# Band attention into a gated feed-forward: a unit's two query tiles laid into the two halves of the partition rows

## The chip, the cores and the metric

The kernel runs on one core of a Trainium2 chip. The metric is the time of one execution in microseconds (us), measured on the device. TensorE is called PE, its weight loads PEld, VectorE DVE, ScalarE ACT, GpSimd POOL, and the engine that issues the DMAs SP.

## What is computed

For 4 batches of 8 heads with 768 positions and 64 dimensions per head, every position attends to the 4 first positions (the sinks) and to itself and the 127 positions ahead of it; then a gated feed-forward runs over the 3072 tokens of 512 values. Everything is float32.

```python
scores = scale * q @ k.T                     # per batch and head, 768 x 768
keep = (pos < n_sink) | ((0 <= rel) & (rel < window))
a = softmax(where(keep, scores, -1e9))
x = (a @ v), heads side by side              # 3072 x 512
out = (sigmoid(x @ w_gate) * (x @ w_val)) @ w_out     # d_ff = 1536
```

## The kernel before, in words

**Units.** The attention is cut into 96 units: `AT` gives three groups of T = 2 query tiles (128 queries each) per batch, and `attend` (line 719) handles one head of one group. A tile's keys are those of its own 128 positions, those of the 128 ahead, and 16 sink columns; `KW` = 144 is one stored key tile with its sinks, so a score tile has 272 columns, or 144 where the tile is the first of its sequence (`n`, line 756). The host hands q and k over transposed, head dimension first.

**Plain and split units.** The first `PLAIN` = 16 units multiply in full float32: each matmul then shows as two records in the trace. The other 80 split each operand into a rounded part (type fp32r, which TensorE multiplies in one pass) and the rest, and add up products of parts. `load` (line 701) brings q and k into the tile `qkT`: a plain unit once, into rows 0 to 63; a split unit twice, into rows 0 to 63 and 64 to 127, so with four DMAs, and one more for v.

**Scores of a split unit** (lines 738 to 749 and 758 to 765). `copy` and `rest` make `qs` (rounded q in the upper 64 rows, the rest of q in the lower 64), `kh` (rounded k in both halves) and `kl` (rest of k in both halves). With all 128 rows contracted, `qs` x `kh` and `qs` x `kl` together hold all four products. So a score tile is two matmuls over 128 rows:

```python
pairs = (qs, kh), (qs, kl)
PE.matmul(sc()[:, 0:n], lhsT=qq()[0:K, t*128 : t*128+128],
          rhs=kk()[0:K, s0 : s0+n], ...)      # K = 64 if plain else 128
```

Each of the two tiles of a unit is a planner operation of its own (line 781) with its own PSUM bank of the ring `a` (`B_a` = 3). After it come mask and row minimum on DVE (`top`), the exponential on ACT (`exp`), the reciprocal of the row sums (`rs`), the multiplication of `P` by it tile by tile (lines 797 to 811), the sink part (`st`, `turned`, `sk`), the transposes of P on TensorE (`turn`), two band cuts on POOL (`split`), and the product with v (`pv`). The result goes to `XH` and `XL`, the rounded part and the rest of x, which hold 6 tiles (`RING`).

**Feed-forward.** `feed` and `feed_part` (lines 1089 and 1119) work on chunks of 2 or 3 tiles (`MT`). Chunk 0 uses the weights in float32; its x lies in the tiles `X0`, which borrow the buffers of `qs`, `kh`, `kl` and `vhl` (line 987). Later chunks use three fp32r products per weight block: matmuls `m<-XH,ws`, `m<-XL,ws` for gate and value, and `o<-ws,gh`, `o<-wol,gh`, `o<-ws,gl` for the output.

**Order.** `Plan` (line 256) is a list scheduler that runs while the kernel is built. Every operation has a priority and, for each engine that could do it, a cost in ns; the plan decides which engine does it, in which order each engine works, and which buffer a tile gets. On TensorE attention operations come first (priority = unit number), feed-forward operations fill the rest (`pe`, from 10000 up), and until 130 us of planned time extra matmuls on the identity (`warm`, `m<-ident`) fill up a stretch that has too little work. The engines then run these fixed orders and wait for one another by semaphores. All instructions of the plan carry line 489, so the groups below are told apart by tile names.

Of the kernel before, what the change touches and what calls it, by code (L numbers as in the profile page):

```python
# [20 lines left out]
NS = 16  # L21
# [27 lines left out]
UPS = 2  # L49
B_vraw = 2  # L50
B_turned = 3
B_qs = 2
B_kh = 2
B_vhl = 3
B_P = 2
B_w = 2
DNG = 0
ADDG = 0
# [15 lines left out]
BUFS = {}  # L74

@with_exitstack
def general(ctx, tc, q, k, v, ident, nsk, win, wres, wol_d, out):

    nc = tc.nc
    B, H, D, S = q.shape  # L80
    NT = S // 128
    DO = out.shape[1]
    NF = len(wres)
# [28 lines left out]
    with tc.For_i(0, B, 1) as b:  # L112
        with tc.For_i(0, H, 1) as h:
# [4 lines left out]
                )  # L118
            )
            qT = c1.tile([D, S], F32, name="gqT")  # L120
            nc.sync.dma_start(
                out=qT, in_=q[bass.ds(b, 1), bass.ds(h, 1)].rearrange("b h d s -> d (b h s)")
            )
            kT = c1.tile([D, S], F32, name="gkT")
            nc.sync.dma_start(
                out=kT.rearrange("d (t p) -> d t p", t=NT),
                in_=k[bass.ds(b, 1), bass.ds(h, 1)].rearrange(
                    "b h d (t p) -> d (b h t) p", t=NT
                )[:, :, 0:128],
            )  # L130
            for t in range(NT):
                sc = c2.tile([128, S], F32, name="g_sc")
                a = c2.tile([128, S], F32, name="g_a")
# [302 lines left out]
def kernel(  # L436
    ctx: ExitStack,
    tc: tile.TileContext,
    q: bass.AP,
    k: bass.AP,  # L440
    v: bass.AP,
    n_sink: bass.AP,
    window: bass.AP,
# [7 lines left out]
    w_gate, w_val, w_out = (  # L451
        w.bitcast(I32).rearrange("r (c w) -> r c w", w=2) for w in (w_gate, w_val, w_out)
    )
    B, H, D, S = q.shape
    DM, DF, _ = w_gate.shape
    DO = w_out.shape[1]
    NC = DM // 128
# [1 line left out]
    SCALE = 1.0 / float(D) ** 0.5  # L459
    NT = S // 128  # L460
    KW = 128 + NS

    keep = ctx.enter_context(tc.tile_pool(name="keep", bufs=1))
    wp = ctx.enter_context(tc.tile_pool(name="wp", bufs=1))
# [39 lines left out]
    def mac(cols):  # L504
        return max(cols * 13 / 12 / 2.4, 104.5) + 2.5

    def dma(prio, ns, fn, r=(), w=()):
        plan.op(prio, [("Q", 460, fn)], r, w, dma=ns)
# [43 lines left out]
    def tile(shape, dtype, tag, bufs, pool=None):  # L552
        return Tile(pool or p1, shape, dtype, tag, bufs)
# [144 lines left out]
            copy(u, H // 2 * D, hi, x, [raw], [(VSHL, i)])  # L698
            rest(u, H // 2 * D, lambda hs=hs: VSHL()[:, hs, D : 2 * D], x, hi, [raw], [(VSHL, i)])

    def load(u, b, h, t0, T, prev, L, vraw, qkT, plain):

        W, k0 = T * 128, (t0 - prev) * 128
        for part, src, o, n in ((0, k, (t0 - prev) * KW, L * KW), (2, q, t0 * 128, W)):
            at = 0 if part else W
            for i in range(1 if plain else 2):
                dma(
                    u, 0.75 * n, lambda i=i, src=src, o=o, n=n, at=at: Q.dma_start(
                        out=qkT()[i * D : i * D + D, at : at + n],
                        in_=src[b, h, :, o : o + n],  # L710
                    ), w=[(qkT, part + 4 * i)],
                )
        dma(
            u, 182.0 * L, lambda: Q.dma_start(
                out=vraw(), in_=v[b, h, k0 : k0 + L * 128].rearrange("(l p) d -> p l d", p=128)
            ), w=[vraw],
        )

    def attend(u, b, h, t0, T, XR):
# [6 lines left out]
            sinks(b, u)  # L726
        plain = u < PLAIN
        vraw = tile([128, L, D], F32, "vraw", BUFS["vraw"])
        qkT = tile([128, W + L * KW], F32, "qkT", BUFS["turned"])
        qT = lambda: qkT()[:, 0:W]  # L730
        kTf = lambda: qkT()[:, W : W + L * KW]
        load(u, b, h, t0, T, prev, L, vraw, qkT, plain)
        kk2, qq2 = [(qkT, 0), (qkT, 4)], [(qkT, 2), (qkT, 6)]
        if plain:
            pairs = ((qT, kTf),)
            qk_reads, qk_ns = [qkT], 4
        else:
            qs = tile([128, W], F32R, "qs", BUFS["qs"])
            kh = tile([128, L * KW], F32R, "kh", BUFS["kh"])
            kl = tile([128, L * KW], F32R, "kl", BUFS["kh"])  # L740
            copy(u, W, qs, qT, qq2, [qs])
            copy(u, L * KW, kh, kTf, kk2, [kh])
            rest(
                u, W, lambda: qs()[D:128], lambda: qT()[D:128], lambda: qs()[D:128],
                qq2 + [qs], [qs],
            )
            rest(u, L * KW, kl, kTf, kh, kk2 + [kh], [kl])
            pairs = (qs, kh), (qs, kl)
            qk_reads, qk_ns = [qs, kh, kl], 2

        P = tile([128, T, KW], F32, "P", BUFS["P"])
        rs = tile([128, 4], F32, "rs", BUFS["P"])
        for t in range(T):
            sc = tile([128, 512], F32, "a", BUFS["a"], ps)
            first = t0 + t == 0
            n = KW if first else KW + 128

            def qk(t=t, sc=sc, n=n):
                s0 = max(t + prev - 1, 0) * KW
                K = D if plain else 128  # L760
                for i, (qq, kk) in enumerate(pairs):
                    PE.matmul(
                        sc()[:, 0:n], lhsT=qq()[0:K, t * 128 : t * 128 + 128],
                        rhs=kk()[0:K, s0 : s0 + n], start=i == 0, stop=i == len(pairs) - 1,
                    )

            def top(t=t, sc=sc, first=first):
                if not first:
                    V.copy_predicated(out=sc()[:, 0:128], mask=tri, data=sc()[:, KW : KW + 128])
                V.tensor_tensor_reduce(  # L770
                    out=P()[:, t], in0=sc()[:, 0:KW], in1=am[min(t0 + t, 2)], op0=ALU.add,
                    op1=ALU.min, scale=-SCALE, scalar=3.0e38, accum_out=negm_all[:, u, t : t + 1],
                )

            def exp(t=t):
                A.activation(
                    out=P()[:, t], in_=P()[:, t], func=AF.Exp, bias=negm_all[:, u, t : t + 1],
                    scale=-1.0, accum_out=rs()[:, t : t + 1],
                )

            plan.op(u, [("PE", 10 + qk_ns * mac(n), qk)], qk_reads, [sc, (P, t)], busy=0.5 if plain else 0.9)
            plan.op(
                u, [("V", 290 if first else 600, top)],
                [sc, (MASKS, 3), (MASKS, min(t0 + t, 2))], [sc, (P, t)],
            )
            plan.op(u, [("A", 460, exp)], [], [(P, t), (rs, t)])
# [7 lines left out]
        plan.op(  # L794
            u, [("V", 120, lambda: V.reciprocal(out=rs()[:, 0:T], in_=rs()[:, 0:T]))], [], [rs]
        )
        for t in range(T):
            plan.op(
                u, [
                    ("V", 390, lambda t=t: V.tensor_scalar(  # L800
                        out=P()[:, t], in0=P()[:, t], scalar1=rs()[:, t : t + 1], scalar2=None,
                        op0=ALU.mult,
                    )),
                    ("A", 320, lambda t=t: A.mul(out=P()[:, t], in_=P()[:, t], mul=rs()[:, t : t + 1])),
                    ("G", 450, lambda t=t: G.tensor_scalar(
                        out=P()[:, t], in0=P()[:, t], scalar1=rs()[:, t : t + 1], scalar2=None,
                        op0=ALU.mult,
                    )),
                ][::-1],
                [rs], [(P, t)],  # L810
            )

        if not plain:
            st = tile([128, T, 2, NS], F32R, "st", BUFS["st"])
            turned = tile([128, T, 2 * NS], F32, "turned", BUFS["st"])
            sk = tile([128, T, 4, 32], F32R, "sk", BUFS["sk"])
            sinkw = lambda: P()[:, :, 128:KW]
            copy(u, 2 * T * NS, lambda: st()[:, :, 0], sinkw, [P], [(st, 0)])  # L820
            rest(
                u, T * NS, lambda: st()[:, :, 1], sinkw, lambda: st()[:, :, 0], [P, (st, 0)], [(st, 1)]
            )
            plan.op(
                u, [("V", 180, lambda: V.transpose(
                    out=turned().rearrange("p t x -> p (t x)"),
                    in_=st().rearrange("p t z x -> p (t z x)").bitcast(F32),
                ))],
                [st], [turned],
            )  # L830
            spread = lambda E: lambda: E.tensor_tensor(
                out=sk(), in0=turned().unsqueeze(2).broadcast_to([128, T, 4, 32]),
                in1=own.unsqueeze(1).unsqueeze(3).broadcast_to([128, T, 4, 32]), op=ALU.mult,
            )
            plan.op(
                u, [("G", pool(W), spread(G)), ("V", vec(W), spread(V))], [turned, OWN], [sk]
            )

        tp = tile([128, 512], F32, "a", BUFS["a"], ps)
# [130 lines left out]
        if h % 2:  # L970
# [8 lines left out]
            for run in runs:  # L979
# [5 lines left out]
                whole = chunk_of[g + run[0]] < WHOLE  # L985
                if whole:
                    X0[c] = tile([128, W], F32, *(
                        (("qs", BUFS["qs"]), ("kh", BUFS["kh"]), ("kl", BUFS["kh"]), ("vhl", BUFS["vhl"]))[c]
                    ))
                    copy(u, W, X0[c], x, [xr], [X0[c]], plain)  # L990
                    continue
# [266 lines left out]
    main.close()  # L1258
    flagged = nc.values_load(total[0:1, 0:1], min_val=0, max_val=512)
    with tc.If(flagged > 0):  # L1260
        general(tc, q, k, v, ident, nsk, win, wres, wol_d, out)


_INS = ["q", "k", "v", "n_sink", "window", "moe_w_gate", "moe_w_val", "moe_w_out"]
_OUTS = [((3072, 512), "float32")]


# [35 lines left out]
```

## Time and profile before

| | |
|---|---|
| time, median of 3 runs | 821.65 us (820.0 to 822.29) |
| time of the profiled execution | 821.27 us |
| its span, first to last instruction | 819.3 us |
| mean granted TensorE clock | 0.988 |
| busy: PE, PEld | 801.7 us, 706.3 us |
| busy: DVE, POOL, ACT | 529.1 us, 470.0 us, 420.1 us |

Matmuls are pipelined: the duration that the trace gives for one runs until its last result is written, while the next one has long begun. What a matmul occupies is read from the distance between the starts of two neighbours. The granted clock is a share of 2.4 GHz.

### The profile page before, as it was taken

What the parts mean: (1) busy time and instruction counts of PE and PEld (TensorE: products, weight loads), DVE (VectorE), ACT (ScalarE), POOL (GpSimd) and SP (SyncE); (2) the same over time, 40 slices, a digit from 0 to 9 for tenths busy, and PEclk for the clock granted to TensorE, in tenths of its full rate; (3) what the DMA queues carried; (4) which work ended last, traced back from release to release, by engine and by line L of the source; (5) the groups of instructions that cost most, each with busy time, mean ns of one, the idle gap of its engine ahead of it and who ended that gap; (6) DMA issues with size and microseconds to landing.
All of it is one profiled execution on the core that took longest, in us unless ns stands there. A gap on an engine that the chain in (4) does not pass through costs nothing.

```text
span 819.3 us, 14819 instructions
## 1 busy us (share of the span) xinstructions
PE 801.7 (98%) x4472; PEld 706.3 (86%) x4472; DVE 529.1 (65%) x1659; ACT 420.1 (51%) x1232; POOL 470.0 (57%) x666
## 2 busy tenths in 40 slices
PE   7999999999999999999999999999999999999997
PEld 5666576789999999999899988899899999999996
DVE  4668787988888888786951499956961495111111
ACT  4667777766677777654730377734640373001001
POOL 3467788787777777664851488755751474111111
PEclk7899999999999999999999999999999999999999
DMA  5567796454454553334341243433441141112112
GB/s 166 152 175 231 206 275 205 110 149 126 130 157 119 144 130 94 107 105 116 103 113 40 66 137 86 134 100 97 104 119 38 50 109 27 48 34 88 40 38 68
DMA packets 101013, 92.93 MB, mean 113 GB/s; under 512 B 47680, under 2 KB 82496, under 8 KB 100928
## 3 DMA queue, kind: packets, MB, share of 16 engines
q1 hardware_dynamic: 100928, 91.93, 40.4%
q8 instruction: 38, 0.62, 0.3%
q14 instruction: 47, 0.39, 0.1%
HBM read 82.45 MB, written 9.44 MB: 112 GB/s over the span
## 4 chain that ended last, share of the span: by engine, by line
PE 67%; DVE 8%; POOL 2%; ACT 2%; DMA 1%; issue 1%; SPq 0%; POOLq 0%; DVEq 0%; ACTq 0%
PE m L489 39%; PE o L489 19%; PE a L489 9%; DVE rs L489 1%; DMA qkT<-in_k_dram 1%; DVE P L489 1%; DVE st L489 1%; DVE gl L489 1%; POOL kl L489 1%; DVE xr L489 1%; DVE a L489 1%; ACT P L489 1%; DVE low L489 1%; DVE th L489 0%; POOL wt L489 0%
## 5 line engine op out<-in xcount | busy, mean ns | idle before, releaser
L489 PE MATMUL m<-XH,ws 128*128 128x384 f32 (+1 forms) x1536 | 399.7, 325 | 0.2 <-DVE th L489 0.2
L489 PEld LDWEIGHTS m<-XH,ws 128*128 128x128 f32 x1536 | 273.9, 188 | 2.9 <-DVE th L489 0.4
L489 PE MATMUL m<-XL,ws 128*128 128x384 f32 (+1 forms) x768 | 247.6, 322 | 0.0
L489 DVE SCALAR_TENSOR_TENSOR th<-th,m 128x384 f32<-128x384 f32 (+1 forms) x108 | 54.6, 505 | 193.5 <-PE m L489 190.3
L489 POOL TENSOR_TENSOR gl<-th,gh 128x384 fp32r<-128x384 f32 (+1 forms) x61 | 61.4, 1006 | 188.9 <-DVE gh L489 183.5
L489 ACT ACTIVATE th<-m 128x384 f32<-128x384 f32 (+1 forms) x108 | 49.1, 455 | 222.5 <-PE m L489 221.5
L489 PEld LDWEIGHTS m<-XL,ws 128*128 128x128 f32 x768 | 144.9, 189 | 2.5
L489 POOL TENSOR_SCALAR_AFFINE_SELECT wt<-wt 128x512 fp32r<-128x512 f32 (+3 forms) x192 | 121.1, 631 | 33.4 <-DVE wt L489 13.7
L489 PE MATMUL o<-ws,gh 128*128 128x512 f32 x264 | 106.4, 403 | 0.0
L489 PE MATMUL o<-ws,gl 128*128 128x512 f32 x264 | 104.3, 395 | 0.7 <-DVE gl L489 0.4
L489 PE MATMUL o<-wol,gh 128*128 128x512 f32 x264 | 103.2, 391 | 0.0
L489 ACT ACTIVATE P<-P,negm_all 128x144 f32<-128x144 f32 x192 | 78.9, 411 | 29.5 <-DVE negm_all L489 24.3
L489 DVE CUSTOM_DVE_ANT_0 P<-a,am 128x144 f32<-128x144 f32 x192 | 58.3, 305 | 7.9 <-PE a L489 2.2
L489 PEld LDWEIGHTS o<-ws,gl 128*128 128x128 f32 x264 | 49.5, 188 | 14.6 <-DVE gl L489 1.8
L489 ACT ACTIVATE P<-P,rs 128x144 f32<-128x144 f32 x114 | 44.1, 410 | 22.5 <-DVE rs L489 22.1
L489 PEld LDWEIGHTS o<-wol,gh 128*128 128x128 f32 x264 | 49.7, 188 | 5.7
L489 PEld LDWEIGHTS o<-ws,gh 128*128 128x128 f32 x264 | 49.7, 188 | 5.2
L489 POOL TENSOR_TENSOR qs<-qkT,qs 64x256 fp32r<-64x256 f32 x57 | 44.4, 779 | 16.0 <-issue 4.5
L489 POOL TENSOR_TENSOR kl<-qkT,kh 128x432 fp32r<-128x432 f32 (+1 forms) x45 | 50.1, 1112 | 3.9 <-ACT kh L489 2.0
L489 PE MATMUL a<-wt,vhl 128*128 128x256 f32 (+1 forms) x216 | 49.2, 330 | 0.5 <-POOL wt L489 0.3
L489 DVE COPY_PREDICATED a<-tri,a 128x128 f32<-128x128 int32 x160 | 45.4, 284 | 6.2 <-PE a L489 5.5
L489 PE MATMUL a<-kh,qs 128*128 128x272 f32 (+1 forms) x160 | 46.5, 295 | 1.1 <-DVE wt L489 0.5
(129 smaller groups left out, 1460.2 us busy)
## 6 DMA issues: line engine op xcount, KB each, us to landing
wol<-wol_d SPq DMA_DIRECT2D x96, 256.0 KB, 2.8
qkT<-in_k_dram SPq DMA_DIRECT2D x120, 108.0 KB, 2.7
qkT<-in_q_dram SPq DMA_DIRECT2D x176, 64.0 KB, 2.4
wst<-in_moe_w_gate_dram SPq DMA_DIRECT2D x12, 512.0 KB, 4.4
wst<-in_moe_w_val_dram SPq DMA_DIRECT2D x12, 512.0 KB, 4.1
wst<-in_moe_w_out_dram SPq DMA_DIRECT2D x12, 512.0 KB, 4.6
vraw<-in_v_dram SPq DMA_DIRECT2D x64, 96.0 KB, 2.3
out_dram<-w SPq DMA_DIRECT2D x23, 256.0 KB, 2.3
```

Of the source, the lines that this page charges most:

```text
L489: return lambda *a, **kw: tc.keep_in_program_order(op(*a, **kw))
```

## The change

One planner operation `qk_` now makes the scores of both tiles of a unit. The host lays out one array `qk`: per batch, head and pair of tiles 128 rows of 400 columns; rows 0 to 63 belong to the first tile of the pair, rows 64 to 127 to the second, and each row holds 128 columns of q, 128 of the preceding keys, 16 of the sinks and 128 of the tile's own keys. One DMA loads it. A split unit makes a rounded part `hi` and a rest `lo` of the whole tile and adds up three products, each over 64 rows, with the two tiles' matmuls issued in turn. The multiplication of `P` by the reciprocal sums is one operation for both tiles (ACT, if chosen, still does it tile by tile). The costs that the planner reckons with change for these and for the sink steps, the ring of `P` has 3 buffers in place of 2, `hi` and `lo` have 3 each, and `X0` borrows one `hi`, one `lo` and two `vhl`.

```diff
-B_qs = 2
-B_kh = 2
+B_hi = 3
-B_P = 2
+B_P = 3
...
-        for part, src, o, n in ((0, k, (t0 - prev) * KW, L * KW), (2, q, t0 * 128, W)):
-            at = 0 if part else W
-            for i in range(1 if plain else 2):
-                dma(... out=qkT()[i * D : i * D + D, at : at + n], in_=src[b, h, :, o : o + n] ...)
+        dma(u, 1.5 * QK, lambda: Q.dma_start(out=qkT(), in_=qk[b, h, t0 // 2]), w=[qkT])
...
-            copy(u, W, qs, qT, qq2, [qs])
-            copy(u, L * KW, kh, kTf, kk2, [kh])
-            rest(u, W, qs()[D:128], qT()[D:128], qs()[D:128], ...)
-            rest(u, L * KW, kl, kTf, kh, kk2 + [kh], [kl])
-            pairs = (qs, kh), (qs, kl)
+            hi = tile([128, QK], F32R, "hi", BUFS["hi"])
+            lo = tile([128, QK], F32R, "lo", BUFS["hi"])
+            copy(u, QK, hi, qkT, [qkT], [hi])
+            rest(u, QK, lo, qkT, hi, [qkT, hi], [lo])
+            pairs = (hi, hi), (hi, lo), (lo, hi)
...
+        SC = [tile([128, 512], F32, "a", BUFS["a"], ps) for _ in range(T)]
+        width = [KW if t0 + t == 0 else KW + 128 for t in range(T)]
+        def qk_():
+            for i, (qq, kk) in enumerate(pairs):
+                for t in range(T):
+                    d = slice(t * D, t * D + D)
+                    PE.matmul(
+                        SC[t]()[:, 0 : width[t]], lhsT=qq()[d, 0:128],
+                        rhs=kk()[d, 128 : 128 + width[t]], start=i == 0, stop=i == len(pairs) - 1,
+                    )
+        plan.op(
+            u, [("PE", 20 + len(pairs) * (4 * width[-1] / 2.4 if plain else mac(width[-1]) + 6), qk_)],
+            [qkT] if plain else [hi, lo], SC + [(P, t) for t in range(T)], ...
+        )
-            plan.op(u, [("PE", 10 + qk_ns * mac(n), qk)], qk_reads, [sc, (P, t)], ...)
...
-        for t in range(T):
-            plan.op(u, [V.tensor_scalar / A.mul / G.tensor_scalar of P()[:, t] by rs()[:, t]], ...)
+        plan.op(
+            u, [("G", pool(T * KW), share(G)), ("A", T * 400, shares), ("V", vec(T * KW), share(V))],
+            [rs], [P],
+        )
...
-                        (("qs", ...), ("kh", ...), ("kl", ...), ("vhl", ...))[c]
+                        (("hi", ...), ("lo", ...), ("vhl", ...), ("vhl", ...))[c]
```

## Rows read from the trace of the kernel before

**Rows 1.** From the page: busy time of each engine with its share of the span and its instructions, and the span in 40 slices with PE's busy tenths and its granted clock.

```profile
PE 801.7 (98%) x4472; PEld 706.3 (86%) x4472; DVE 529.1 (65%) x1659; ACT 420.1 (51%) x1232; POOL 470.0 (57%) x666
PE   7999999999999999999999999999999999999997
PEclk7899999999999999999999999999999999999999
```

**Rows 2.** Busy time by stage: from and to (us), length, then for PE, PEld, DVE, ACT and POOL busy us (instructions), PE's granted clock, the DMA engines' busy share, GB/s.

```profile
0.00:40.00 40.00, 34.99 (x155) 24.71 (x156) 21.32 (x88) 21.73 (x51) 17.80 (x34) 0.79 0.55 157
40.00:100.00 60.00, 60.00 (x267) 36.59 (x268) 45.20 (x125) 44.62 (x107) 43.69 (x51) 1.00 0.71 202
100.00:160.00 60.00, 56.94 (x264) 41.51 (x263) 51.62 (x118) 45.74 (x103) 48.98 (x55) 1.00 0.70 205
160.00:360.00 200.00, 199.48 (x1327) 187.11 (x1326) 170.64 (x582) 137.37 (x455) 151.54 (x230) 1.00 0.48 128
360.00:600.00 240.00, 236.94 (x1325) 218.12 (x1324) 173.39 (x557) 125.03 (x395) 144.56 (x218) 1.00 0.36 99
600.00:819.00 219.00, 213.33 (x1142) 198.26 (x1141) 66.94 (x194) 45.64 (x124) 63.46 (x81) 1.00 0.21 58
```

**Rows 3.** PE's waits, longest first in total: who waited for whom, us in total, times, longest us.

```profile
PE a L489 <- POOL P L489: 2.0, 3, 1.7
PE a L489 <- DVE wt L489: 1.8, 3, 0.7
...
PE a L489 <- POOL kl L489: 0.8, 1, 0.8
```

**Rows 4.** The last kind of weight load from memory, as SP issues it: number, ns of an issue at least/median/at most, first and last start in us.

```profile
L489 SPq DMA_DIRECT2D wst<-in_moe_w_out_dram x12: 340/428/562, 8.7 to 136.9; - x12
```

**Rows 5.** Timeline of PE in the split stage: start (us), duration (us), operation, output from inputs, rows*columns of the weights, moving operand, number.

```profile
200.09 0.23 PE L489 MATMUL a<-kh,qs 128*128 128x144 f32 x1
200.16 0.28 PE L489 MATMUL a<-kl,qs 128*128 128x144 f32 x1
200.27 0.44 PE L489 MATMUL o<-ws,gh 128*128 128x512 f32 x1
200.55 0.39 PE L489 MATMUL o<-wol,gh 128*128 128x512 f32 x1
200.78 0.39 PE L489 MATMUL o<-ws,gl 128*128 128x512 f32 x1
...
207.57 0.28 PE L489 MATMUL a<-kh,qs 128*128 128x272 f32 x1
207.70 0.28 PE L489 MATMUL a<-kl,qs 128*128 128x272 f32 x1
207.82 0.28 PE L489 MATMUL m<-XH,ws 128*128 128x256 f32 x1
```

**Rows 6.** All score matmuls of the split units by shape (busy us, mean ns of one), and the last unit's product with the sinks (ns at least/median/at most, first and last start in us).

```profile
L489 PE MATMUL a<-kh,qs 128*128 128x272 f32 x136 | 41.2, 307 | 1.1 <-DVE wt L489 0.5 <-DVE negm_all L489 0.4
L489 PE MATMUL a<-kh,qs 128*128 128x144 f32 x24 | 5.5, 229 | 0.0
L489 PE MATMUL a<-sk,vshl x80: 276/280/286, 123.3 to 685.7; 128*128 128x256 f32 x80
```

**Rows 7.** Timeline of PE in the plain stage, at a granted clock of 1.00; equal neighbours are merged, with their number at the end.

```profile
44.45 0.71 PE L489 MATMUL m<-ident 128*128 128x128 f32 x4
45.09 0.72 PE L489 MATMUL a<-qkT 64*128 64x272 f32 x2
45.74 0.71 PE L489 MATMUL m<-ident 128*128 128x128 f32 x4
46.29 0.60 PE L489 MATMUL a<-ident,P 128*128 128x128 f32 x4
46.73 0.39 PE L489 MATMUL m<-ident 128*128 128x128 f32 x2
...
58.43 1.18 PE L489 MATMUL a<-qkT 64*128 64x272 f32 x4
59.54 0.70 PE L489 MATMUL m<-kl,ws 128*128 128x256 f32 x2
```

**Rows 8.** Weight loads of 128 and of 64 rows: number, busy us, mean ns.

```profile
L489 PEld LDWEIGHTS a<-kh,qs 128*128 128x128 f32 x160 | 30.2, 188 | 4.3 <-DVE wt L489 1.1 <-issue 1.0 <-ACT ws L489 0.4
L489 PEld LDWEIGHTS a<-qkT 64*128 64x128 f32 x64 | 10.1, 197 | 8.6 <-issue 3.3 <-PE a L489 1.5 <-DMA qkT<-in_q_dram 1.2
```

**Rows 9.** The splitting of q and k and the multiplication of P: number, busy us, mean ns of one.

```profile
L489 ACT CAST qs<-qkT 128x256 fp32r<-128x256 f32 x70 | 28.2, 402 | 9.7 <-PE a L489 5.8 <-POOL wt L489 2.3 <-DMA qkT<-in_k_dram 0.9
L489 ACT CAST kh<-qkT 128x432 fp32r<-128x432 f32 x49 | 26.9, 549 | 1.2 <-PE a L489 1.2
L489 ACT CAST kh<-qkT 128x288 fp32r<-128x288 f32 x20 | 8.6, 429 | 0.2 <-PE a L489 0.2
...
L489 POOL TENSOR_TENSOR qs<-qkT,qs 64x256 fp32r<-64x256 f32 x57 | 44.4, 779 | 16.0 <-issue 4.5 <-POOL vhl L489 3.4 <-POOL wt L489 2.3
L489 POOL TENSOR_TENSOR kl<-qkT,kh 128x432 fp32r<-128x432 f32 x33 | 39.4, 1193 | 3.0 <-ACT kh L489 1.5 <-DMA vraw<-in_v_dram 0.4
L489 POOL TENSOR_SCALAR P<-P,rs 128x144 f32<-128x144 f32 x49 | 36.4, 744 | 12.5 <-DVE rs L489 8.6 <-PE m L489 0.9 <-DMA vraw<-in_v_dram 0.9
L489 POOL TENSOR_TENSOR kl<-qkT,kh 128x288 fp32r<-128x288 f32 x12 | 10.7, 890 | 0.9 <-ACT kh L489 0.5
```

**Rows 10.** Issues of the loads of q and k: number, KB of each, median us from issue to landing.

```profile
qkT<-in_k_dram SPq DMA_DIRECT2D x120, 108.0 KB, 2.7
qkT<-in_q_dram SPq DMA_DIRECT2D x176, 64.0 KB, 2.4
```

More of the change, by code (lines that the diff above doesn't have):

```diff
@@ L76, in general @@
 @with_exitstack
-def general(ctx, tc, q, k, v, ident, nsk, win, wres, wol_d, out):
+def general(ctx, tc, qk, v, ident, nsk, win, wres, wol_d, out):
     nc = tc.nc
-    B, H, D, S = q.shape
+    B, H, S, D = v.shape
     NT = S // 128
@@ L120, in general @@
             qT = c1.tile([D, S], F32, name="gqT")
-            nc.sync.dma_start(
-                out=qT, in_=q[bass.ds(b, 1), bass.ds(h, 1)].rearrange("b h d s -> d (b h s)")
-            )
             kT = c1.tile([D, S], F32, name="gkT")
[L125 to L130, printed above, removed]
+            for x, o in ((qT, 0), (kT, 128 + 128 + NS)):
+                for t in range(2):
+                    nc.sync.dma_start(
+                        out=x.rearrange("d (n t x) -> d t n x", t=2, x=128)[:, t],
+                        in_=qk[
+                            bass.ds(b, 1), bass.ds(h, 1), :, t * D : t * D + D, o : o + 128
+                        ].rearrange("b h n d x -> d (b h n) x"),
+                    )
             for t in range(NT):
@@ L438 @@
     tc: tile.TileContext,
-    q: bass.AP,
-    k: bass.AP,
+    qk: bass.AP,
     v: bass.AP,
@@ L453 @@
     )
-    B, H, D, S = q.shape
+    B, H, S, D = v.shape
     DM, DF, _ = w_gate.shape
@@ L461 @@
     KW = 128 + NS
+    QK = 128 + KW + 128
     keep = ctx.enter_context(tc.tile_pool(name="keep", bufs=1))
@@ L699, in sinks, with load @@
             rest(u, H // 2 * D, lambda hs=hs: VSHL()[:, hs, D : 2 * D], x, hi, [raw], [(VSHL, i)])
-    def load(u, b, h, t0, T, prev, L, vraw, qkT, plain):
-        W, k0 = T * 128, (t0 - prev) * 128
-        for part, src, o, n in ((0, k, (t0 - prev) * KW, L * KW), (2, q, t0 * 128, W)):
-            at = 0 if part else W
-            for i in range(1 if plain else 2):
[L707 to L712, printed above, removed]
+    def load(u, b, h, t0, L, k0, vraw, qkT):
+        dma(u, 1.5 * QK, lambda: Q.dma_start(out=qkT(), in_=qk[b, h, t0 // 2]), w=[qkT])
         dma(
@@ L728, in attend @@
         vraw = tile([128, L, D], F32, "vraw", BUFS["vraw"])
[L729 to L733, printed above, removed]
+        qkT = tile([128, QK], F32, "qkT", BUFS["turned"])
+        load(u, b, h, t0, L, k0, vraw, qkT)
         if plain:
-            pairs = ((qT, kTf),)
-            qk_reads, qk_ns = [qkT], 4
-        else:
-            qs = tile([128, W], F32R, "qs", BUFS["qs"])
-            kh = tile([128, L * KW], F32R, "kh", BUFS["kh"])
-            kl = tile([128, L * KW], F32R, "kl", BUFS["kh"])
-            copy(u, W, qs, qT, qq2, [qs])
-            copy(u, L * KW, kh, kTf, kk2, [kh])
[L743 to L746, printed above, removed]
-            rest(u, L * KW, kl, kTf, kh, kk2 + [kh], [kl])
-            pairs = (qs, kh), (qs, kl)
-            qk_reads, qk_ns = [qs, kh, kl], 2
+            pairs = ((qkT, qkT),)
+        else:
+            hi = tile([128, QK], F32R, "hi", BUFS["hi"])
[3 more added lines that the diff above has]
+            pairs = (hi, hi), (hi, lo), (lo, hi)
@@ L751, in attend @@
         P = tile([128, T, KW], F32, "P", BUFS["P"])
         rs = tile([128, 4], F32, "rs", BUFS["P"])
-        for t in range(T):
[L754 to L765, printed above, removed]
+        SC = [tile([128, 512], F32, "a", BUFS["a"], ps) for _ in range(T)]
@@ new lines, in attend @@
+        width = [KW if t0 + t == 0 else KW + 128 for t in range(T)]
[9 more added lines that the diff above has]
+            u, [("PE", 20 + len(pairs) * (4 * width[-1] / 2.4 if plain else mac(width[-1]) + 6), qk_)],
+            [qkT] if plain else [hi, lo], SC + [(P, t) for t in range(T)], busy=0.5 if plain else 0.9,
+        )
@@ L767, in top @@
+        for t in range(T):
+            sc, first = SC[t], t0 + t == 0
             def top(t=t, sc=sc, first=first):
@@ L779, in exp @@
                 )
-            plan.op(u, [("PE", 10 + qk_ns * mac(n), qk)], qk_reads, [sc, (P, t)], busy=0.5 if plain else 0.9)
             plan.op(
@@ L796, in attend, with shares @@
         )
-        for t in range(T):
[L798 to L811, printed above, removed]
+        share = lambda E: lambda: E.tensor_tensor(
+            out=P(), in0=P(), in1=rs()[:, 0:T].unsqueeze(2).broadcast_to([128, T, KW]), op=ALU.mult
+        )
+        def shares():
+            for t in range(T):
+                A.mul(out=P()[:, t], in_=P()[:, t], mul=rs()[:, t : t + 1])
+        plan.op(
+            u, [("G", pool(T * KW), share(G)), ("A", T * 400, shares), ("V", vec(T * KW), share(V))],
+            [rs], [P],
+        )
         if not plain:
@@ L819, in attend @@
             sinkw = lambda: P()[:, :, 128:KW]
-            copy(u, 2 * T * NS, lambda: st()[:, :, 0], sinkw, [P], [(st, 0)])
-            rest(
-                u, T * NS, lambda: st()[:, :, 1], sinkw, lambda: st()[:, :, 0], [P, (st, 0)], [(st, 1)]
-            )
+            high, low_ = lambda: st()[:, :, 0], lambda: st()[:, :, 1]
+            plan.op(
+                u, [
+                    ("A", 215, lambda: A.copy(out=high(), in_=sinkw())),
+                    ("V", 385, lambda: V.tensor_copy(out=high(), in_=sinkw())),
+                ],
+                [P], [(st, 0)],
+            )
+            less = lambda E: lambda: E.tensor_tensor(
+                out=low_(), in0=sinkw(), in1=high().bitcast(F32), op=ALU.subtract
+            )
+            plan.op(u, [("G", 335, less(G)), ("V", 390, less(V))], [P, (st, 0)], [(st, 1)])
             plan.op(
-                u, [("V", 180, lambda: V.transpose(
+                u, [("V", 240, lambda: V.transpose(
                     out=turned().rearrange("p t x -> p (t x)"),
@@ L835, in attend @@
             plan.op(
-                u, [("G", pool(W), spread(G)), ("V", vec(W), spread(V))], [turned, OWN], [sk]
+                u, [("G", 660, spread(G)), ("V", 590, spread(V))], [turned, OWN], [sk]
             )
@@ L987, in attend @@
                     X0[c] = tile([128, W], F32, *(
-                        (("qs", BUFS["qs"]), ("kh", BUFS["kh"]), ("kl", BUFS["kh"]), ("vhl", BUFS["vhl"]))[c]
+                        (("hi", BUFS["hi"]), ("lo", BUFS["hi"]), ("vhl", BUFS["vhl"]), ("vhl", BUFS["vhl"]))[c]
                     ))
@@ L1260 @@
     with tc.If(flagged > 0):
-        general(tc, q, k, v, ident, nsk, win, wres, wol_d, out)
-_INS = ["q", "k", "v", "n_sink", "window", "moe_w_gate", "moe_w_val", "moe_w_out"]
+        general(tc, qk, v, ident, nsk, win, wres, wol_d, out)
+_INS = ["qk", "v", "n_sink", "window", "moe_w_gate", "moe_w_val", "moe_w_out"]
 _OUTS = [((3072, 512), "float32")]
@@ L1276 @@
     arrays, args = {}, []
-    for name in _INS:
-        a = inputs[name]
-        if name in "qk":
-            a = a.transpose(0, 1, 3, 2)
-        if name == "k":
-            t = a.reshape(*a.shape[:3], -1, 128)
-            a = _np.concatenate([t, _np.broadcast_to(t[..., :1, :NS], (*t.shape[:4], NS))], axis=4)
-            a = a.reshape(*a.shape[:3], -1)
+    q, k = (inputs[x].transpose(0, 1, 3, 2) for x in "qk")
+    k = k.reshape(*k.shape[:3], -1, 128)
+    sinks = k[..., :1, :NS]
+    rows = [
+        _np.concatenate(
+            [q[..., t * 128 : t * 128 + 128], k[..., max(t - 1, 0), :], sinks[..., 0, :], k[..., t, :]],
+            axis=3,
+        )
+        for t in range(k.shape[3])
+    ]
+    qk = _np.stack(
+        [_np.concatenate(rows[t : t + 2], axis=2) for t in range(0, len(rows), 2)], axis=2
+    )
+    for name in _INS:
+        a = qk if name == "qk" else inputs[name]
         a = _np.ascontiguousarray(a)
```

## The prediction

> **What bounds the kernel now.** I read the page's busy times first: PE is busy for 98% of the span [rows 1]. Matmuls overlap in that view, so I took three more views before believing it. By stage [rows 2], PE stands idle for 5.0 us ahead of 40 us and for 3.1 us between 100 and 160 us; from 160 us on it is idle for 0.5, 3.1 and 5.7 us, and most of the last is the end, after the final matmul (the last slice of PE is at 7 tenths [rows 1]). Its list of waits is short: the largest entry is 2.0 us in all [rows 3]. The starts on the timeline stand back to back: one score matmul starts at 207.57, the next at 207.70, the one behind at 207.82 [rows 5]. So from 160 us on, at a granted clock of 1.00, the time is the sum of what TensorE streams and loads, and 1 ns of PE work more or less per unit moves the end by that. DVE and POOL are busy for 85% and 76% of 160 to 360 us, but nobody on PE waits long for them. Ahead of 160 us the loading of the weights also sets a pace: it goes on until 136.9 us [rows 4].
>
> **The change, part by part.**
>
> *Scores of the 80 split units, before.* Two matmuls of 272 columns take 0.25 us from the first's start to the start of what follows. Two of 144 take 0.18 us (200.09 to 200.27), and the matmul behind them takes 0.28 us (to 200.55) where its like takes 0.23 (200.55 to 200.78), since its weight load is late: 0.23 us together [rows 5]. There are 136 score tiles of the first kind and 24 of the second [rows 6]: 136 x 0.25 + 24 x 0.23 = 39.5 us.
>
> *What leaving and re-entering the full array costs.* The split stage so far holds only matmuls over 128 rows. The change puts six matmuls over 64 rows into each of the 80 units. The plain stage shows what that does, since its scores are over 64 rows already [rows 7]. Four records of 272 columns in one visit take 58.43 to 59.54, 1.11 us; two take 45.09 to 45.74, 0.65 us. So two records stream in 0.46 us, and each visit pays 0.19 us on top. On the other side of the border: four records of 128 columns with like neighbours take 46.29 to 46.73, 0.44 us; four that stand between two visits take 44.45 to 45.09, 0.64 us, so 0.20 us on top. A visit therefore costs 0.39 us, half of it in the visit and half in the matmuls around it: twice the array runs empty (about 0.09 us), and twice the first weight load lies open (about 0.10 us). I take 0.39 us per unit, since `qk_` makes both tiles in one visit: 80 x 0.39 = 31.2 us. The bounds are nothing, if fp32r matmuls of one pass didn't pay it (no row shows them over 64 rows), and the full sum.
>
> *The six matmuls inside a visit.* The two tiles of a product use different rows and different banks. If they stream at once, a product costs what one tile of 272 columns does, 0.125 us: 3 x 0.125 = 0.375 us a unit, 30.0 us in all. No row shows two halves at work together, so bounds: if nothing overlaps, 6 x 0.125 = 0.75 us a unit, 60.0 us. Between these lies the weight load. A load of 64 rows is recorded no shorter than one of 128, 197 against 188 ns [rows 8], and behind a short matmul the next starts only 0.11 us later, when its load is done (200.16 to 200.27, where 144 columns stream in 0.07, as from 200.09 to 200.16) [rows 5]. If the six loads go one after another, the sixth matmul starts 0.55 us after the first and streams for 0.125: 0.675 us a unit, 54.0 us. I take the lower end, because the halves share neither rows, weights nor banks, and the rows on loads are of one and the same part of the array; both other values stay in the range.
>
> By the rows' one load after another the sum would be 24.0 us higher than by loads side by side. The Trainium skill, "TensorEngine Tiling (Array Packing)", section "Key Properties", says that different tiles of the array can load weights and multiply in parallel; by that rule the sum is the lower one. No row here shows it. The same section says that a change of tiling mode drains the engine, which speaks against this change; the trace agrees, with 0.39 us a visit.
>
> *Sum on TensorE.* 31.2 + 30.0 - 39.5 = +21.7 us.
>
> *The 16 plain units.* Their 64-row visits exist already, some for one tile and some for two [rows 7]; now each unit has one. Where two visits become one, 0.39 us goes, and the second tile's first record may run beside the first tile's second, 0.23 us. At most that is 16 x 0.62 = 9.9 us. But it lies ahead of 100 us, where PE fills gaps with `m<-ident` or waits for weights, which come in until 136.9 us [rows 4]. I take -1 us, bounds 0 and -9.9.
>
> *Splitting.* ACT's two copies, 402 + 549 ns (429 for the short k), become one of 400 columns, about 0.52 us between its rows; POOL's 779 + 1193 ns (890) become one of about 1.1 us [rows 9]. That frees some 0.4 us of ACT and 0.8 of POOL or DVE per unit. The two multiplications of P (744 ns each on POOL) become one of 288 columns, by the 890 ns of the like subtraction: about 0.6 us less where POOL does them. All of it runs beside PE's work, so it can only give back PE's waits: 0.5 us in 160 to 360, 3.1 in 360 to 600, 3.1 in 100 to 160 [rows 2]. I take -1 us of these 6.7; if ACT, DVE or POOL were late again, PE would wait for P or wt as now [rows 3].
>
> *Loads.* A split unit had two of k and two of q, now one of 128 x 400 x 4 bytes, 200 KB in place of 2 x (108 + 64) [rows 10]. Three issues a unit fewer on SP, hidden on both sides: PE has no wait on these loads after the first units, and the DMA engines are half idle from 160 us on. A plain unit loads 200 KB in place of 172, 0.4 MB in all, some 2 us at 205 GB/s [rows 2], spread over 100 us beside other work: nothing.
>
> *Buffers.* `qk_` needs two of the three `a` banks at once, and both parts of a buffer of P. Queued behind it on PE stands feed-forward work, which the plan puts ahead while banks are taken. Attention ends at 685.7 us [rows 6], with over 100 us of feed-forward left, so later scores cost nothing until that lead is gone. `X0` leaves one `vhl` buffer until chunk 0 ends, so v of a unit is split only after the product of the unit before; at worst PE waits a few times for about a microsecond between 100 and 160 us. I take 0, bounds 0 and +4.
>
> *Together:* +21.7 - 1 - 1 = +19.7. The profiled execution took 821.27 us (span 819.3 and some 2 around it); the median, 821.65, lies 0.4 us above. 821.3 + 19.7 = 841 us.
>
> **The rivals.**
>
> *A, loads one after another.* For it: the 0.11 us spacing [rows 5] and loads that don't shrink with the rows [rows 8]. Against: those rows never show two parts of the array. 31.2 + 54.0 - 39.5 - 2 = +43.7: 865 us.
>
> *B, the halves don't overlap at all,* so the packing doesn't do what it is written for: 31.2 + 60.0 - 39.5 - 2 = +49.7: 871 us.
>
> *C, faster: a visit is free for fp32r matmuls of one pass.* The place is the border of each of the 80 visits. Then 30.0 - 39.5 - 2 = -11.5: 810 us. It decides from the point where a visit costs less than (39.5 - 30.0 + 2)/80 = 0.14 us, about a third of the 0.39 seen. Against it: the price is the same for every neighbour in the plain stage, at 128 or 272 columns.
>
> *D, part of a visit's cost is hidden,* the open loads but not the emptying: 0.2 us a visit, 80 x 0.2 = 16.0 + 30.0 - 39.5 - 2 = +4.5: 826 us.
>
> **How the numbers follow.** Forecast 0.50, A 0.25, B 0.12, C 0.07, D 0.06. The predicted time is the forecast's, 841 us; with the bounds of the small terms it reaches from 832 to 847. To hold 8 in 10, the range must take in A and the near side of B, and leaves out C, D and the rest of B: 830 to 870 us. A measurement of this kernel tells about 0.3%, 2.5 us, from no change. Faster by more: C, 0.07. Within: the low side of D, 0.02. Slower: the rest, 0.91.
>
> **What would show it.** The timeline of a split unit should hold six records of 64*128; right is that the two of a product start within some 0.01 us, the products about 0.125 apart, the matmul ahead is longer by about 0.09, and the first record behind by about 0.09 with a late second. Records 0.11 apart mean A, 0.125 apart B, no lengthening of the neighbours C. PE should stay above 97% busy, ACT and POOL should lose some 30 and 60 us of splitting. The prediction is wrong if six 64-row records and their surroundings take less than 0.6 us.

## The result and the profile after

The kernel after takes 826.3 us in the median of 8 runs (823.7 to 828.8), the kernel before 822.0 beside it: a ratio of 1.0056, 95% interval 1.0035 to 1.0077. The forecast was 841 us and a range of 830 to 870: slower was right, but +4.3 us came where +19.7 was forecast. The profiled execution, whose trace is read below, was the slowest of the eight: 828.8 us, with a span of 827.0.

Busy times and slices from its page answer to [rows 1]:

```profile
PE 812.2 (98%) x4678; PEld 699.4 (85%) x4678; DVE 503.9 (61%) x1596; ACT 391.3 (47%) x1140; POOL 433.4 (52%) x622
...
PE   8999999999999999999999999999999999999996
...
PEclk9999999999999999999999999999999999999999
```

The same stages as in [rows 2], with the same columns:

```profile
0.00:40.00 40.00, 36.46 (x224) 26.94 (x225) 27.39 (x106) 24.44 (x63) 20.90 (x38) 1.00 0.68 204
40.00:100.00 60.00, 60.00 (x299) 38.34 (x298) 48.35 (x125) 45.21 (x107) 43.22 (x46) 1.00 0.70 214
100.00:160.00 60.00, 58.83 (x310) 44.75 (x309) 49.95 (x125) 46.45 (x115) 49.38 (x55) 1.00 0.62 184
160.00:360.00 200.00, 200.00 (x1322) 176.85 (x1321) 146.12 (x510) 117.69 (x380) 124.77 (x197) 1.00 0.35 98
360.00:600.00 240.00, 238.50 (x1360) 211.53 (x1361) 164.78 (x539) 113.08 (x358) 134.94 (x208) 0.99 0.30 83
```

PE is still what sets the time. Between 160 and 360 us POOL drops from 151.5 to 124.8 us and ACT from 137.4 to 117.7, by the lighter splitting and multiplication of P, and PE gains nothing from it: it was busy before and is busy now.

One split unit on PE's timeline, as in [rows 5], and the weight loads of the same stretch:

```profile
201.69 0.28 PE L487 MATMUL m<-XL,ws 128*128 128x256 f32 x1
201.81 0.28 PE L487 MATMUL m<-XH,ws 128*128 128x256 f32 x1
202.02 0.39 PE L487 MATMUL a<-hi 64*128 64x144 f32 x2
202.19 0.35 PE L487 MATMUL a<-lo,hi 64*128 64x144 f32 x2
202.30 0.37 PE L487 MATMUL a<-hi,lo 64*128 64x144 f32 x2
202.60 0.39 PE L487 MATMUL m<-XH,ws 128*128 128x256 f32 x1
202.82 0.28 PE L487 MATMUL m<-XL,ws 128*128 128x256 f32 x1
```

```profile
202.02 0.19 PEld L487 LDWEIGHTS a<-hi 64*128 64x128 f32 x2
202.13 0.19 PEld L487 LDWEIGHTS a<-lo,hi 64*128 64x128 f32 x2
202.24 0.20 PEld L487 LDWEIGHTS a<-hi,lo 64*128 64x128 f32 x2
```

The last full-array matmul ahead is 0.09 us longer than its like (201.81 to 202.02, 0.21 against 0.12), the visit takes 0.58 us (202.02 to 202.60), and the first behind is 0.10 us longer (0.22 against 0.12). That is 0.77 us in all, where the forecast's 0.39 + 3 x 0.125 make 0.765; the median of the 80 visits is 0.57 us, so the unit shown is a typical one. The view merges equal neighbours: two loads, one for each half, show as one of 0.19 us, which is what a single one takes, so they go side by side. The Trainium skill, "TensorEngine Tiling (Array Packing)", section "Key Properties", says that different tiles of the array can load weights and multiply in parallel, and this trace agrees.

Where the time went shows in the span of the later chunks' first matmuls, before and after (ns at least/median/at most, first and last start):

```profile
L489 PE MATMUL m<-XH,ws x1536: 276/334/469, 151.9 to 808.9; 128*128 128x384 f32 x144, 128*128 128x256 f32 x48
```

```profile
L487 PE MATMUL m<-XH,ws x1536: 273/335/668, 140.9 to 815.3; 128*128 128x384 f32 x144, 128*128 128x256 f32 x48
```

Chunk 1, the first of these chunks, begins 11.0 us earlier; from there to the last of these matmuls the kernel takes 674.4 us in place of 657.0, 17.4 more. So a loss of nearly the forecast's size stands beside a gain ahead of it that the forecast had put at 1 us.

### The profile page after: what moved, and what is told of

It reads as the page before. It is cut to its first block, busy times and chain, and to the rows that moved or that the text cites. A ratio compares the mean times of both kernels' runs of the same rounds, so it can differ in the third digit from the quotient of the medians.

```text
span 827.0 us, 14467 instructions
## 1 busy us (share of the span) xinstructions
PE 812.2 (98%) x4678; PEld 699.4 (85%) x4678; DVE 503.9 (61%) x1596; ACT 391.3 (47%) x1140; POOL 433.4 (52%) x622
## 4 chain that ended last, share of the span: by engine, by line
PE 81%; DMA 2%; DVE 1%; POOL 1%; ACT 1%; issue 0%; POOLq 0%; DVEq 0%
PE m L487 46%; PE o L487 23%; PE a L487 12%; DMA wst<-in_moe_w_gate_dram 2%; DVE ws L487 1%; POOL wt L487 0%; POOL lo L487 0%; ACT ws L487 0%; POOL vhl L487 0%; ACT wst L487 0%; DVE wt L487 0%; DVE low L487 0%; DVE vhl L487 0%; DVE xr L487 0%; ACT P L487 0%
## 5 line engine op out<-in xcount | busy, mean ns | idle before, releaser
L487 PE MATMUL m<-XH,ws 128*128 128x384 f32 (+1 forms) x1536 | 404.1, 330 | 0.0
L487 POOL TENSOR_TENSOR gl<-th,gh 128x384 fp32r<-128x384 f32 (+1 forms) x57 | 56.8, 997 | 165.5 <-DVE gh L487 157.9
L487 POOL TENSOR_SCALAR_AFFINE_SELECT wt<-wt 128x512 fp32r<-128x512 f32 (+3 forms) x192 | 118.3, 617 | 34.0 <-DVE wt L487 12.2
L487 PE MATMUL o<-ws,gh 128*128 128x512 f32 x264 | 108.7, 412 | 0.0
L487 POOL TENSOR_TENSOR lo<-qkT,hi 128x400 fp32r<-128x400 f32 x70 | 75.1, 1072 | 40.7 <-ACT hi L487 33.7
L487 ACT CAST hi<-qkT 128x400 fp32r<-128x400 f32 x61 | 32.0, 526 | 34.7 <-PE a L487 31.5
L487 ACT ACTIVATE P<-P,rs 128x144 f32<-128x144 f32 x114 | 40.9, 407 | 9.0 <-DVE rs L487 9.0
L487 PEld LDWEIGHTS a<-wt,vhl 128*128 128x128 f32 x216 | 39.3, 190 | 6.1 <-POOL wt L487 0.5
```

The source lines that it names most:

```text
L487: return lambda *a, **kw: tc.keep_in_program_order(op(*a, **kw))
```

## The experiments

The theory after the result (theory 1): the price of the visits is as forecast, and the plain units won back the rest. Its rivals: the split units' lighter splitting won it back (theory 2); the changed costs that the planner reckons with did; the order that the planner happened to find did. All ratios are to the kernel before, run in the same session.

### The two halves of the change apart

`plain_new` changes the plain units alone, `split_new` the split units alone (a flag chooses the old or the new code of each):

```diff
-PLAIN_NEW = 1      # after: both 1, before: both 0
-SPLIT_NEW = 1
+PLAIN_NEW = 1      # plain_new; split_new: 0
+SPLIT_NEW = 0      # plain_new; split_new: 1, with B_hi = 2
```

> Only the 16 plain units are changed (one load, both tiles' scores in one visit, one multiplication of P); the 80 split units keep their 128-row scores, their costs in the plan and their buffers. Theory 1, the price of a visit is as forecast and the kernel won back some 13 us before chunk 1 by the plain units: 806 to 812 us. Theory 2, what was won back comes from the split units' lighter splitting: 819 to 822 us.

> Only the split units are changed (hi and lo with 2 buffers in place of 3, for room); the plain units are as before. Theory 1: 838 to 844 us, the forecast's sum without the plain units. Theory 2: 825 to 830 us.

Measured: `plain_new` 812.2 us (ratio 0.987, 0.983 to 0.991), `split_new` 841.6 us (1.025, 1.020 to 1.029; of its five runs one took 832.9 us, the one whose trace is kept, and the others 841.3 to 845.8, so this median is less firm). The split units cost about 20 us by themselves, the plain units give back about 10: theory 1. But the parts add up to +10, not to +4.3.

`after_hi2` asks if `split_new`'s missing third buffer explains that, `after_no_share` what the common multiplication of P is worth:

```diff
-B_hi = 3
+B_hi = 2           # after_hi2
-SHARE_PLAIN = SHARE_SPLIT = 1
+SHARE_PLAIN = SHARE_SPLIT = 0   # after_no_share: P tile by tile
```

> The kernel after with 2 buffers of hi and lo in place of 3, as split_new has. The two halves of the change gave +19.9 and -9.5 us by themselves and +4.4 together. If the third buffer makes the difference of 6 us: 830 to 834 us. If the parts help each other in another way: 825 to 828 us.

> The kernel after with the multiplication of P tile by tile in all units, as before. If the common multiplication costs, as plain_new against plain_no_share says (+4 us): 819 to 823 us. If it matters in the plain units' order alone by chance: 824 to 829 us.

Measured: 825.5 us (1.004, 1.003 to 1.006) and 826.7 us (1.005, 1.004 to 1.007). Neither matters in the kernel after, so the gap between the sum of the parts and the whole is not explained by them.

### The price of a visit, and of streaming at once

`visit64` is the kernel before, in the same order, with the second product of each split score tile over 64 rows:

```diff
-                K = D if plain else 128
                 for i, (qq, kk) in enumerate(pairs):
+                    K = D if plain or i else 128
```

> The kernel before, in the same order of instructions; the second product of each split score tile contracts rows 0 to 63 alone (it leaves out rest of q times rest of k). So 160 visits of one 64-row matmul each and nothing else. At the 0.39 us of the plain stage per visit: 821.6 + 62 = 884 us. If fp32r matmuls of one pass changed between row counts for nothing: 822 us.

Measured: 869.3 us (1.056, 1.051 to 1.061), +47.5 us and not the +62 of the first reading. One of its 160 visits on PE's timeline:

```profile
207.46 0.29 PE L489 MATMUL a<-kh,qs 128*128 128x272 f32 x1
207.68 0.39 PE L489 MATMUL a<-kl,qs 64*128 64x272 f32 x1
207.99 0.50 PE L489 MATMUL o<-ws,gh 128*128 128x512 f32 x1
208.33 0.39 PE L489 MATMUL o<-wol,gh 128*128 128x512 f32 x1
208.56 0.40 PE L489 MATMUL o<-ws,gl 128*128 128x512 f32 x1
```

The three steps from 207.46 to 208.33 take 0.87 us; at 0.125, 0.125 and 0.23 they would take 0.48. So 0.39 us again, and rival C is out. Since both kernels issue the same instructions in the same order, the distances between starts can be set against each other one by one: those at the 160 visits grow by 58.5 us in all (0.37 each), all others shrink by 10.4. The second number is what waits give back when PE gets more to do: 9.9 of it lie in 37 steps, most of them ahead of a matmul that opens the work of another engine, such as P, wt or gl. PE's idle time shows only part of it: between 160 and 600 us the steps shrink by 7.6 us, while the idle time falls by 3.6, from 0.5 and 3.1 us [rows 2] to nothing:

```profile
160.00:360.00 200.00, 200.00 (x1206) 172.56 (x1205) 150.10 (x519) 125.91 (x415) 134.32 (x202) 1.00 0.41 116
360.00:600.00 240.00, 240.00 (x1238) 209.69 (x1237) 155.85 (x505) 113.28 (x355) 130.24 (x201) 1.00 0.32 92
```

`one_half` and `tile_by_tile` are the kernel after with other operands or another order of the six products:

```diff
-                    d = slice(t * D, t * D + D)
+                    d = slice(0, D) if not plain else slice(t * D, t * D + D)   # one_half
-            for i, (qq, kk) in enumerate(pairs):
-                for t in range(T):
+            for t in range(T):                                                  # tile_by_tile
+                for i, (qq, kk) in enumerate(pairs):
```

> The kernel after in the same order, but both tiles' split scores are taken from rows 0 to 63 (tile 1 is computed from tile 0's q and k), so nothing of them can overlap. If the two halves stream at once in the kernel after, six steps of 0.125 us take the place of three: 80 x 0.375 = +30 us, 852 to 858 us, less what hides in waits. If they don't: 826 us.

> The kernel after, with a split unit's six products ordered tile by tile in place of in turn; the plan and everything else is the same. If the two halves stream at once when in turn (and only the last of tile 0 beside the first of tile 1 here): five steps of 0.125 us in place of three, 80 x 0.25 = +20 us, 846 us. If nothing overlapped in the kernel after: 826 us.

Measured: `one_half` 854.0 us (1.040, 1.038 to 1.042), 27.7 more than after: the halves do stream at once, and rival B is out. `tile_by_tile` took 828.3 us (1.008, 1.006 to 1.011), 2 more than after and not 20. This fits neither reading. Its program issues a unit's three products of the first tile (rows 0 to 63) and then the three of the second (rows 64 to 127), and its trace still shows pairs. For a unit whose first tile has 144 columns (the view gives the shape of the first of two merged records):

```profile
201.01 0.40 PE L487 MATMUL a<-hi 64*128 64x144 f32 x2
201.18 0.36 PE L487 MATMUL a<-lo,hi 64*128 64x144 f32 x2
201.29 0.37 PE L487 MATMUL a<-hi,lo 64*128 64x144 f32 x2
201.59 0.39 PE L487 MATMUL m<-XH,ws 128*128 128x256 f32 x1
```

The visit takes 0.58 us, as in the kernel after. In each of the 80 units the second record starts 0.01 us behind the first and is the second tile's first product: it starts beside the first tile's first, past two that stand ahead of it in the program. So the order was no test of the overlap, and `one_half` was.

### What the plain units gave back

All in the plain units alone, with the split units of before:

```diff
-        if SHARE_PLAIN: one multiplication of P for both tiles      # plain_new
+        tile by tile                                               # plain_no_share
...
-("PE", 20 + 4 * width[-1] / 2.4, qk_)                               # plain_new
+("PE", sum(10 + 4 * mac(n) for n in width), qk_)                   # plain_old_cost
...
-d = slice(t * D, t * D + D)                                         # plain_no_share
+d = slice(0, D)                                                     # plain_one_half
...
-("PE", 10 + 4 * mac(n), qk)                                         # before
+("PE", 10 + 4 * n / 2.4 / 2, qk)                                    # plan_cost_only
```

> The kernel plain_new without the common multiplication of P (tile by tile again in the plain units). Theory S1, the plain units' gain is the shorter scores on TensorE: 810 to 814 us. Theory S2, it is what the planner believes of their cost: 810 to 814 us. Theory S3, it is the multiplication of P: 819 to 823 us.

> The kernel plain_new (sharing of P in plain units kept), but the planner reckons with the old cost of the plain scores, 2 x (10 + 4 products), about 1.0 us in place of 0.47. S1: 810 to 814 us, since the instructions are as short as before in plain_new. S2: 819 to 823 us. S3: 810 to 814 us.

> The kernel before; only the planner's cost of a plain score tile is halved, so the order of the work changes and no instruction of a unit does. S1 and S3: 819 to 824 us. S2: 810 to 815 us.

> The kernel plain_no_share in the same order of instructions, but the plain units' two score tiles both come from rows 0 to 63 (tile 1 is computed from tile 0's q and k), so they stream one after the other in one visit; loads, plan and the rest are as there. If the gain of the plain units is that their two tiles stream at once, 16 x 0.46 = 7.4 us come back of 13.4: 814 to 817 us. If it is the loads or the order: 807 to 810 us.

Measured: `plain_no_share` 808.2 us (0.984, 0.982 to 0.985), faster than any of the three theories had it, and S3 is out; `plain_old_cost` 812.3 us (0.989, 0.988 to 0.991), so S2, the planner's costs, is out; `plan_cost_only` 817.7 us (0.996, 0.994 to 0.998), between the two readings: its order alone is worth some 4 us, as much as the trifles below. `plain_one_half` took 811.2 us (0.987, 0.983 to 0.991). Its order is that of `plain_no_share`, but the tiles stream one after the other, and it is 3 us slower, not 7. The two intervals overlap, and the kernel before stood at 823.4 us beside the one and at 821.6 beside the other, so 1 to 3 us of the gain, not firmly told from none, are the streaming at once.

The traces show what the plain scores take of PE. In the kernel after, each plain unit is one visit of four records, here 0.66 us (57.27 to 57.93), where four records took 1.11 us before [rows 7]:

```profile
57.27 0.73 PE L487 MATMUL a<-qkT 64*128 64x272 f32 x4
57.93 1.13 PE L487 MATMUL o<-ws,th 128*128 128x512 f32 x2
```

Added up from the first record of a visit to the next other matmul, the plain scores took 22.3 us in 24 visits before and 11.0 us in 16 visits after. Between 40 and 100 us, at a granted clock of 1.00 and with PE busy for 60.00 of 60 us in both kernels, it was 1.22 us a unit before and 0.66 after.

`one_load` keeps the single load and makes the scores two operations of the plan again; `one_op` keeps the old loads and makes them one:

```diff
-plan.op(u, [("PE", ..., qk_)], [qkT], SC + [(P, t) for t in range(T)])    # plain_no_share
+for t in range(T): plan.op(u, [("PE", 10 + 4 * mac(width[t]), lambda t=t: qk_([t]))], ...)  # one_load
-for t in range(T): plan.op(u, [("PE", 10 + 4 * mac(n), qk)], ...)         # before
+plan.op(u, [("PE", ..., both)], qk_reads, SC + ...)                       # one_op
```

> The kernel plain_no_share, but a plain unit's two score tiles are two operations of the plan again, as before, each with the old cost; the loads stay single. Theory L, the gain of the plain units comes from the single loads: 807 to 812 us. Theory O, it comes from scores as one operation (one visit, two tiles ready at once): 818 to 823 us.

> The kernel before; a plain unit's two score tiles are one operation of the plan (one visit, both from rows 0 to 63, nothing overlaps), the loads of q and k stay two. Theory L: 818 to 823 us. Theory O: 809 to 814 us.

Measured: `one_load` 822.8 us (1.001, 0.998 to 1.004, with runs from 816.4 to 830.6), `one_op` 819.5 us (0.997, 0.995 to 0.999). Neither alone gives the gain; theories L and O fall both. Their plain scores took 19.1 and 17.0 us of PE, those of `plain_one_half` 16.1 and of `plain_no_share` 11.3. So PE time is not the whole of it: `one_op` and `plain_one_half` differ by 0.9 us in it and by 8.3 us in time. They differ in the loads and in the order.

### What an order is worth by chance

Two trifles in the plan, for the kernel before (`jiggle`), the kernel after and, one of them, `plain_no_share`:

```diff
-            plan.op(u, [("A", 460, exp)], [], [(P, t), (rs, t)])
+            plan.op(u, [("A", 470, exp)], [], [(P, t), (rs, t)])     # a
-LAT = 180.0
+LAT = 190.0                                                          # b
```

> The kernel before; one planned cost is changed by a trifle (the exponential 470 in place of 460 ns), so the planner finds another order for the same instructions. It shows how much of a few us an order is worth by chance (theory J: such a change alone moves the time by 4 us or more; otherwise 820 to 824 us).

> As jiggle_a, with another trifle (LAT 190 in place of 180 ns). Theory J: further than 4 us from 822; otherwise 820 to 824 us.

> The kernel after with the trifle of jiggle_a (exponential 470 ns in the plan). If the order is a lottery for the kernel after as for the one before (817.3 and 813.4 for 821.6): anywhere from 818 to 830 us; the mean over orders, not one order, is then what the change is worth. If only the kernel before had drawn badly: 824 to 828 us.

> The kernel after with the trifle of jiggle_b (LAT 190). The same two readings: 818 to 830 us, or 824 to 828 us.

> The kernel plain_no_share with LAT 190. If its 808 us is the worth of the packed plain scores: 806 to 811 us. If it too had drawn well: 811 to 817 us, beside 813.4 for the kernel before with LAT 190.

| order | before | after | plain_no_share |
|---|---|---|---|
| as it was | 822.0 | 826.3 | 808.2 |
| a | 817.3 (0.995, 0.993 to 0.997) | 824.9 (1.003, 1.001 to 1.005) | |
| b | 813.4 (0.990, 0.987 to 0.993) | 827.0 (1.006, 1.004 to 1.008) | 807.1 (0.983, 0.978 to 0.987) |

The ratios are to the kernel before in its own order. That order was the worst of three. The kernel after moves by only 2.1 us under the same trifles, and `plain_no_share` by 1.1. Against the kernel before under the same trifle, the change costs 4.3, 7.6 and 13.6 us, 8.5 in the mean.

The two halves of the change show in the traces whatever the order (one execution of each kernel, the span read from `m<-XH,ws` as above):

| plain units | split units | kernels | chunk 1 begins at | from there to the last `m<-XH,ws` |
|---|---|---|---|---|
| old | old | before, `jiggle_a`, `jiggle_b`, `plan_cost_only` | 146.4 to 155.7 | 657.0, 655.9, 648.8, 658.1 |
| half changed | old | `one_load`, `one_op` | 149.0, 148.3 | 656.1, 657.1 |
| new | old | `plain_new`, `plain_no_share`, `plain_jb`, `plain_old_cost` | 139.8 to 144.5 | 655.1 to 658.1 |
| old | new | `split_new` | 146.3 | 673.3 |
| new | new | after, `after_ja`, `after_jb`, `after_hi2`, `after_no_share` | 135.8 to 140.9 | 674.4 to 677.7 |

New plain units let chunk 1 begin sooner, by 9.3 us in the mean with old split units; new split units add some 18 us behind that point (26.5 from `jiggle_b`, whose chunk 1 begins last, to `after_jb`).

The low clock at the start [rows 2] cost the kernel before nothing that shows. `visit64` has the same instructions in the same order as the kernel before, with its first visit behind 100 us, and a granted clock of 1.00 in the first 40 us in place of 0.79:

```profile
0.00:40.00 40.00, 37.65 (x155) 26.23 (x156) 21.40 (x88) 21.59 (x51) 17.67 (x34) 1.00 0.54 158
```

Its matmuls still reach 100 us within 0.1 us of those of the kernel before. And of the 83 runs of the kernel before beside the experiments, the 14 at a mean clock of 0.998 or 0.999 took 823.9 us in the median, the 69 at 0.985 to 0.989 took 821.7.

## Why the prediction was wrong

*Scores and visits, right.* 0.77 us a unit as forecast. In orders as it was and b the kernel after takes 826.6 us in the mean and `plain_no_share` 807.7, so the split units cost 19.0 us; the forecast had 21.7 - 1 = 20.7. `split_new` by itself gave 19.6 against the kernel before in its own order and 24.0 against the mean of its three orders, so that it comes so near is in part luck. Loads went side by side, so rival A is out, and `one_half` put a price on rival B.

*Waits, a little small.* The forecast let 1 us of the new work vanish in waits and read 6.7 us of idle time as the bound; in `visit64` 10.4 us of 58.5 vanished. A wait that is shorter than the tail of the matmul ahead doesn't show in the busy time. ACT lost 28.8 us of work, as forecast (30), POOL only 36.6 (60); neither shows in the time.

*The plain units, the step that failed.* The text had "-1 us, bounds 0 and -9.9", since PE there "fills gaps with `m<-ident` or waits for weights, which come in until 136.9 us". Measured: -10.0 us in the mean of orders as it was (-13.8) and b (-6.3). The term was worked out and then all but struck off as hidden. The trace shows it in the time: the plain scores take 11.3 us less of PE (22.3 to 11.0), and chunk 1 begins 11.0 us sooner, although PE has more `m<-ident` to do ahead of it (164 records for 118). That the bound came so near is luck: it counted 16 visits saved, and it was 8 (24 to 16); it let 0.23 us of a unit run beside the other tile, and it was 0.45 where both tiles have 272 columns (1.11 to 0.66).

The argument took the loading of the weights for the pace-maker. In the kernel after the last of the same 36 loads of 512 KB starts 6.4 us earlier, in `plain_old_cost` 13.4:

```profile
L487 SPq DMA_DIRECT2D wst<-in_moe_w_out_dram x12: 327/341/424, 7.6 to 130.5; - x12
L497 SPq DMA_DIRECT2D wst<-in_moe_w_out_dram x12: 340/341/537, 7.5 to 123.5; - x12
```

So no fixed supply from memory set their end, and their end alone did not set the start of chunk 1 either: in `plain_old_cost` it is at 144.5 us, later than in the kernel after.

How the time saved on PE becomes time of the kernel is only in part known. 1 to 3 us of the gain are the two tiles streaming at once (`plain_one_half`). The rest needs the single load and the single operation together, or came with the order that they led to; no run tells these apart, and this stays open.

*The draw of the order, not in the forecast at all.* The kernel before is 4.4 us slower in its own order than in the mean of the three (822.0 against 817.6). The parts in means, 19.0 - 10.0 = +9.0, less these 4.4 are +4.6, and measured was +4.3. That they meet proves little, since both parts are differences of the same three kernels; that the order counts is shown by the trifles themselves. Nor do the halves run alone add up in means (24.0 - 5.4 = +18.6 against the 817.6), with one order of each; this stays open too.

Rival D named 826 us, but for a cheaper visit, and the visit is paid in full: that it hit the time is luck.

## What to carry to other kernels

Price a change of the array's row count like an instruction: here 0.39 us each time, against 0.125 us for the product that it saved, so the change paid where the work was over 64 rows already (`plain_no_share`, 808 us, beats both kernels; with order b 807) and lost where 128 rows had been full. Where a list scheduler writes the order, a trifle can move the time by as much as the change: run two or three orders of both kernels before a few us are put down to it. Before a loading stage is taken for a pace-maker, and a saving beside it struck off, see whether it ends earlier when the work beside it gets shorter.

## What the hardware showed beside it

Matmuls on different halves of the rows don't start in the order of the program: in `tile_by_tile` the fourth started beside the first, and the visit took the same 0.58 us in either order. In the profiled execution of the kernel after, the mean granted clock was 0.83 in two stretches of 10 us, so part of each ran at 1.2 in place of 2.4 GHz; shortly ahead of each fall PE had been idle for 1.5 us:

```profile
465.00:475.00 10.00, 8.51 (x45) 7.21 (x44) 6.39 (x21) 6.07 (x18) 6.92 (x11) 0.83 0.59 181
655.00:665.00 10.00, 8.50 (x42) 7.38 (x40) 6.72 (x23) 6.14 (x18) 6.65 (x11) 0.83 0.49 152
```

The four runs of this kernel with a mean clock of 0.994 or 0.995 took 826.5 to 828.8 us, the four with 0.997 or 0.998 took 823.7 to 826.1.
